# A fused attention and MLP kernel: one store of 128 rows a block, groups gated on the DMA turn, later squares, later casts of v, two more units of filler

## The chip, the cores and the metric

The kernel runs on one core of one Trainium2 chip. The metric is the device time of one execution in microseconds (us); smaller is better. The core has a matmul engine (PE, its weight loads are shown as PEld), a vector engine (DVE), an activation engine (ACT), GpSimd (POOL) and a sync engine (SP). Here SP issues every DMA, in its own order. "Clock" is the PE clock that the chip granted, as a share of full speed.

Runs carry a state. A run more than 1.5% above the fastest run of the same kernel counts as slow; a single run on one core is "unknown". On the chip of the first experiments the kernel before had three slow runs of seven (333 to 336 us), so medians over all its runs mislead there.

## The reference, cut to what matters

```python
# q, k, v: (8 batches, 8 heads, 576 rows, 64)
A, Bm, C = sm(q, k_lm), sm(q_lm, k_lm), sm(q_lm, k)       # landmarks: means of 18 rows
Z = Bm.T / (norm1(Bm) * norm_inf(Bm) + 1e-6)
for _ in range(6): Z = 2 * Z - Z @ Bm @ Z
x = (A @ Z @ C @ v)                                       # heads side by side: (8, 576, 512)
xn = (x - mean(x)) / sqrt(var(x) + 1e-6) * g_ln
out = x + relu(xn @ w_ch1) @ w_ch2                        # 512 -> 2048 -> 512
```

## The kernel before

The 4608 rows are 36 blocks of 128 rows, and 4 blocks are a group. The MLP of a group is 64 matmuls of 128x512 into "psh" (first product) and 64 into "pso" (second product). It is written as a generator; `fill(n)` takes n of its matmuls as filler between the small matmuls of the attention of later batches. Batches 0 and 1 go alone; then come four sets: batch 2, batches 3 and 4, batches 5 and 6, batch 7.

A block's way: its rows are made on DVE (`xblk`, with their sum); POOL makes the negative mean (`negm`) and the centred rows (`xn`); SP turns these by a DMA transpose into `xnT`, the operand of the first product. ACT takes the squares (`junk`) for the deviation, which is only needed when the second product is evicted.

Other names in the views: `stg` is a piece of q, k or v as loaded, `nat` and `natv` its casts to 16 bits (`natv` of v); POOL sums `nat` into `asum` and `s`; from DVE's sums `part` PE makes the landmarks (`psl`), which ACT copies out (`lm`); `psec` and `pscv` are products of the attention with them, `psn` is a step of the iteration for Z, and `psy` (from `zcbd`) gives the rows.

```python
def block_done(j):                          # groups 2 and up
    later.append(lambda: mean_of(j, pool))
    later.append(lambda: center(j, pool) ...)      # ends in the DMA transpose
    squares.append(lambda: square(j))              # one is taken out per step
    if u == 3: squares.append(lambda: deviations(g))   # ends in ln_ready.add(g)

def store(j, ot, cols):                     # two stores of 64 rows a block
    for i in range(2):
        b, c = divmod(2 * j + i, NJ)
        half = ot[ds(64 * i, 64), cols]
        to = out[b].rearrange("(t j) f -> j t f", j=NJ)[c][:, cols]
        nc.sync.dma_start(out=to, in_=half)

def mlp():
    for g in range(NGRP):
        ...
        while g > 1 and g not in ln_ready: yield False    # no filler until then
        ... 64 matmuls into psh, Relu on ACT ...
        ... 64 matmuls into pso, eviction on DVE, store ...
```

(Cut and joined for reading; "..." marks the cuts.) The 64 rows of a half block lie 9 rows apart in the output, and the two halves start in different places, sometimes in different batches.

The softmax here doesn't subtract the row's maximum and nothing guards it: scores larger than these inputs give would overflow.

Of the kernel before, what the change touches and what calls it, by code (L numbers as in the profile page):

```python
# [20 lines left out]
def kernel(  # L21
# [10 lines left out]
    nc = tc.nc  # L32
# [11 lines left out]
    NJ = 9  # L44
# [685 lines left out]

        yield from rows_of(bs, ea, zcbd)

    ln_ready = {0}
    rowsum, variances, rstds, xn_of = {}, {}, {}, {}
    mlp_at, uncentered = [0], {}
    later, squares, negms = [], [], {}

    def settle():
        while later:
# [2 lines left out]
    def block_done(j):  # L742
        g, u = divmod(j, 4)
        if g == 0:
            mean_of(j, dve)
            center(j, scalar if u % 2 == 0 else dve)
        elif g == 1:
            mean_of(j, dve)
            later.append(lambda: center(j, scalar))
        else:  # L750
            later.append(lambda: mean_of(j, pool))
            later.append(lambda: center(j, pool) if g <= mlp_at[0] + 1
                         else uncentered.setdefault(g, []).append(j))
        squares.append(lambda: square(j))
        if u == 3:
            if g == 1:
                later.append(lambda: ln_ready.add(1))
            squares.append(lambda: deviations(g))

    def mean_of(j, engine):  # L760
        negms[j] = mstat.tile([P, 1], FP32, name="negm", tag="negm", bufs=16)
# [3 lines left out]
    def center(j, engine):  # L765
        g, u = divmod(j, 4)
        xn_of[j] = xn = mxn.tile([P, DM], FP16, name="xn", tag="xn")
        if engine is scalar:
            act(xn[:], x_blk[j][:], AF.Identity, bias=negms[j][:], scale=1.0)
        elif engine is dve:  # L770
            dve.tensor_scalar(out=xn[:], in0=x_blk[j][:], scalar1=negms[j][:],
                              scalar2=None, op0=ALU.add)
        else:
            pool.tensor_scalar(out=xn[:], in0=x_blk[j][:], scalar1=1.0, scalar2=negms[j][:],
                               op0=ALU.mult, op1=ALU.add)
        if g < 2:
            return
        if u == 0:
            xnTs[g] = mxnT.tile([P, KCH, 512], FP16, name="xnT", tag="xnT")
        keep(nc.sync.dma_start_transpose(out=xnTs[g][:, :, ts(u, P)], in_=xn_of.pop(j)[:]))  # L780

    def square(j):
        g, u = divmod(j, 4)
# [6 lines left out]
    def deviations(g):  # L790
        lnv = mstat.tile([P, 4], FP32, name="lnv", tag="lnv")
        act(lnv[:], variances.pop(g)[:], AF.Ln, bias=eps_ln[:], scale=1.0 / DM)
        rstds[g] = mstat.tile([P, 4], FP32, name="rstd", tag="rstd")
        act(rstds[g][:], lnv[:], AF.Exp, scale=-0.5)
        ln_ready.add(g)

    def store(j, ot, cols):
        for i in range(2):
            b, c = divmod(2 * j + i, NJ)
            half = ot[ds(64 * i, 64), cols]  # L800
            to = out[b].rearrange("(t j) f -> j t f", j=NJ)[c][:, cols]
            nc.sync.dma_start(out=to, in_=half)

    xnTs = {}

# [19 lines left out]
    def mlp():  # L825
        for g in range(NGRP):
            mlp_at[0] = g
            hT = mhT.tile([P, MCH, 512], FP16, name="hT", tag="hT")
            if g == 0:
                for m0, u in ([(m, 0) for m in range(0, 12, 2)] + [(m, 2) for m in range(0, 12, 2)]  # L830
                              + [(m, u) for u in (0, 2) for m in (12, 14)]):
                    for t in {(0, 0): (0, 1), (8, 0): (2,), (10, 0): (3,)}.get((m0, u), ()):
                        transpose_block(0, t)
                        yield True
                    psh = psM.tile([P, 2, 256], FP32, name="psh", tag="pm")
                    for m in range(2):
                        for c in range(KCH):
                            MM(psh[:, m, :], w1_16[:, c, ts(m0 + m, P)],
                               xnTs[0][:, c, ds(P * u, 256)],
                               start=(c == 0), stop=(c == KCH - 1), skip=True)  # L840
                            if c == 1 or (c == 3 and m == 0):
                                yield True
                    act(hT[:, m0:m0 + 2, ds(P * u, 256)], psh[:], AF.Relu)
                    yield True
            else:
                while g == 1 and g not in xnTs:
                    if g in ln_ready:
                        for _ in transposes(g):
                            yield True
                    else:  # L850
                        yield False
                while g > 1 and g not in ln_ready:
                    yield False
                xnT = xnTs.pop(g)
                for j in uncentered.pop(g + 1, ()):
                    center(j, pool)
                for m in range(MCH):
                    psh = psM.tile([P, 512], FP32, name="psh", tag="pm")
                    for c in range(KCH):
                        MM(psh[:], w1_16[:, c, ts(m, P)], xnT[:, c, :],  # L860
                           start=(c == 0), stop=(c == KCH - 1))
                        if c < KCH - 1:
                            yield True
                    act(hT[:, m, :], psh[:], AF.Relu)
                    yield True
            tr = None
            for u in range(4):
                j = 4 * g + u
                x = x_blk.pop(j)
                ot = mout.tile([P, DM], FP32, name="ot", tag="ot")  # L870
                parts = 2 if j == NBLK - 1 else 1
                n = DM // parts
                for part in range(parts):
                    pso = psM.tile([P, n], FP32, name="pso", tag="pm")
                    for m in range(MCH):
                        MM(pso[:], hT[:, m, ts(u, P)], w2_16[:, m, ts(part, n)],
                           start=(m == 0), stop=(m == MCH - 1))
                        if m < MCH - 1:
                            yield True
                        if g == 0 and u >= 2 and m % 8 == 3:  # L880
                            if 1 in ln_ready and 1 not in xnTs:
                                tr = transposes(1)
                            if tr is not None:
                                next(tr, None)
                                yield True
                    dve.scalar_tensor_tensor(out=ot[:, ts(part, n)], in0=pso[:],
                                             scalar=rstds[g][:, u:u + 1], in1=x[:, ts(part, n)],
                                             op0=ALU.mult, op1=ALU.add)
                    store(j, ot, ts(part, n))
                    yield True  # L890
            if tr is not None:
                for _ in tr:
                    yield True
# [68 lines left out]
    def prepare(c, casts, jobs):  # L962
        for _ in range(casts):
            if c.casts and (c.parts[c.casts[0]][0] == "v" or len(c.n16) < 8):
                c.next_cast()
                while sum(len(x.stg) for x in sets) < (3):
                    left = [x for x in sets if x.loads]
                    if not left:
                        break
                    left[0].next_load()  # L970
        for _ in range(jobs):
            c.next_job()

    for _ in range(6):
# [1 line left out]

    fills = {"scores of k": 4, "gram": 5, "iteration": 4,
             "product": 5, "zc": 4, "rows": 6}
    def a_square():
        if squares:  # L980
            squares.pop(0)()

    n = 0
    for what in a1:
        fill(fills[what])
        settle()
        if what in ("iteration", "product"):
            a_square()
        if what in ("product", "zc", "rows"):
            n += 1  # L990
            prepare(sets[0], 1, 1 if n > 3 else 0)
    while len(sets[0].jobs) > 1:
        prepare(sets[0], 1, 1)
        fill(6)
    fill(16)

    steps = [[(10, 0), (12, 1)] + 6 * [(6, 1)] + [(8, 1)] + 5 * [(6, 0)]]
    steps += [[(6, 0), (8, 0), (12, 0), (12, 0), (6, 0), (6, 0), (5, 0), (5, 0), (5, 0), (5, 0), (8, 0)] + 3 * [(6, 0)] + 7 * [(7, 1)]]
    steps += [[(12, 0), (14, 1), (16, 1), (16, 1)] + 6 * [(9, 1)] + [(10, 1)] + 10 * [(8, 1)]]
    steps += [[(15, 0), (18, 0)] + 6 * [(12, 0)] + [(12, 0)] + 5 * [(12, 0)]]  # L1000
    for c, after, plan in zip(sets, sets[1:] + [None], steps):
        while c.jobs:
            prepare(c, 1, 1)
            fill(5 if c is sets[1] else 8)
        for (count, jobs), _ in zip(plan, attention2(c.bs, c)):
            fill(count)
            settle()
            a_square()
            if after:
                prepare(after, 1, jobs)  # L1010
    settle()
    while squares:
        a_square()
    for _ in stream:
        pass

# [29 lines left out]
```

## Time and profile before

| | before |
|---|---|
| median of its first 3 runs | 329.57 us (328.91 to 330.02) |
| span of the profile | 327.9 us |
| PE busy | 312.7 us, 95% |
| mean PE clock | 0.989 |
| last eviction to the end | 324.29 to 327.9: 3.6 us |

### The profile page before, as it was taken

To read this page: it belongs to the slowest core of one execution; us is meant where nothing else is said; L and a number is where in the kernel's file an instruction comes from. 1 tells how busy PE (TensorE), PEld (TensorE's weight loads), DVE (VectorE), ACT (ScalarE), POOL (GpSimd) and SP (SyncE) were. 2 spreads that over 40 slices of the span, in tenths; PEclk is the share of its full clock that TensorE was granted. 3 is DMA by queue.
4 is the path that set the end of the run, shared out by engine and by line. 5 is a ranking of instruction groups with operands and counts; after the bars stand their busy time and mean duration, and the time that the engine had idled before them with its cause. 6 is when DMAs were issued, how large, how long until landed. Compare 5 with 4: busy or idle time off the path is not lost.

```text
span 327.9 us, 7900 instructions
## 1 busy us (share of the span) xinstructions
PE 312.7 (95%) x3248; PEld 157.5 (48%) x3248; DVE 147.7 (45%) x392; ACT 153.9 (47%) x301; POOL 126.6 (39%) x194
## 2 busy tenths in 40 slices
PE   8789999899977989999999999999999999999994
PEld 8568654444432534544454445444444444444443
DVE  2667249678782415799366346431232210010012
ACT  2466853587043671567505644583048316305600
POOL 4389879708994796448043011600010300000000
PEclk9999999999995999999999999999999999999999
DMA  7999999559959993933086003520341124032023
GB/s 265 395 386 385 386 389 281 161 109 388 200 133 292 381 246 88 209 113 65 10 213 162 0 18 80 98 35 2 71 98 25 33 67 93 2 79 50 2 56 72
DMA packets 38700, 50.32 MB, mean 153 GB/s; under 512 B 17540, under 2 KB 17800, under 8 KB 38664
## 3 DMA queue, kind: packets, MB, share of 16 engines
q1 hardware_dynamic: 38664, 49.82, 53.6%
q8 instruction: 25, 0.41, 0.6%
q14 instruction: 11, 0.09, 0.1%
HBM read 36.70 MB, written 9.44 MB: 141 GB/s over the span
## 4 chain that ended last, share of the span: by engine, by line
PE 77%; POOL 6%; DMA 5%; DVE 5%; issue 2%; ACT 2%; SPq 1%; POOLq 0%
PE psh L73 35%; PE pso L73 31%; DMA stg<-in_k_dram 2%; PE psy L73 2%; POOL asum L67 2%; PE psn L73 2%; PE pscv L73 2%; DMA xnT<-xn 2%; POOL nat L67 1%; POOL natv L67 1%; DMA stg<-in_q_dram 1%; DVE xblk L67 1%; PE psec L73 1%; DVE part L67 1%; SPq L780 1%
## 5 line engine op out<-in xcount | busy, mean ns | idle before, releaser
L73 PE MATMUL psh<-xnT,w 128*128 128x512 f16 (+1 forms) x640 | 136.3, 360 | 2.0 <-DMA xnT<-xn 2.0
L73 PE MATMUL pso<-w,hT 128*128 128x512 f16 (+1 forms) x592 | 134.5, 375 | 0.0
L67 ACT ACTIVATE hT<-psh 128x512 f16<-128x512 f32 x144 | 85.0, 598 | 89.4 <-PE psh L73 88.8
L73 PEld LDWEIGHTS <-w 128*128 128x128 f16 x640 | 59.2, 98 | 60.5 <-issue 7.3
L73 PEld LDWEIGHTS <-hT 128*128 128x128 f16 x592 | 56.5, 98 | 58.1 <-issue 1.8
L67 DVE SCALAR_TENSOR_TENSOR ot<-pso,rstd,xblk 128x512 f32<-128x512 f32 (+1 forms) x37 | 27.1, 732 | 71.7 <-PE pso L73 68.4
L67 POOL CAST nat<-stg 128x1152 f16<-128x1152 f32 x28 | 31.6, 1145 | 33.4 <-DMA stg<-in_q_dram 30.0
L67 ACT ACTIVATE junk<-xblk,negm 128x512 f16<-128x512 f32 x36 | 25.9, 721 | 30.1 <-POOL negm L67 29.9
L67 POOL TENSOR_SCALAR negm<-rowsum 128x1 f32<-128x1 f32 x28 | 5.3, 190 | 76.8 <-DVE xblk L67 67.6
L67 DVE SCALAR_TENSOR_TENSOR xblk<-psy,rcpd 128x512 f32<-128x512 f32 (+1 forms) x40 | 27.6, 691 | 2.7 <-DVE rcpd L67 0.5
L67 DVE SCALAR_TENSOR_TENSOR st<-st,psn 128x128 f16<-128x128 f16 (+2 forms) x36 | 11.4, 316 | 38.3 <-PE psn L73 38.3
L67 POOL CAST natv<-stg 128x1152 f16<-128x1152 f32 x16 | 18.4, 1161 | 12.1 <-DMA stg<-in_v_dram 12.0
L67 POOL TENSOR_SCALAR xn<-xblk,negm 128x512 f16<-128x512 f32 x28 | 19.2, 692 | 2.0 <-DMA xnT<-xn 0.9
L67 DVE STREAM_TRANSPOSE xT<-nat 128x576 uint32<-128x576 uint32 x24 | 18.4, 768 | 0.0
L67 DVE TENSOR_REDUCE part<-xT 128x32 f16<-128x576 f16 x26 | 18.3, 745 | 0.1
L67 DVE RECIPROCAL rcpd<-psy 128x8 f32<-128x8 f32 (+1 forms) x40 | 8.1, 202 | 20.9 <-PE psy L73 20.8
L73 PE MATMUL psy<-zcbd,ea 128*128 128x260 f16 (+1 forms) x80 | 15.6, 276 | 0.6 <-DVE zcbd L67 0.5
L73 PEld LDWEIGHTS <-st 32*32 32x32 f16 x448 | 5.7, 89 | 16.7 <-issue 11.8
L67 POOL TENSOR_TENSOR asum<-asum 128x256 f32<-128x256 f32 (+1 forms) x22 | 13.0, 591 | 1.7
L67 POOL TENSOR_TENSOR asum<-nat 128x512 f32<-128x512 f16 x11 | 12.7, 1154 | 0.9
L73 PEld LDWEIGHTS <-ea 128*128 128x128 f16 (+1 forms) x80 | 7.2, 100 | 10.9 <-issue 2.6
L67 ACT ACTIVATE ec<-psec 128x576 f16<-128x576 f32 x12 | 8.9, 808 | 7.3 <-PE psec L73 7.3
(101 smaller groups left out, 210.3 us busy)
## 6 DMA issues: line engine op xcount, KB each, us to landing
stg<-in_q_dram SPq DMA_DIRECT2D x16, 576.0 KB, 7.4
stg<-in_k_dram SPq DMA_DIRECT2D x16, 576.0 KB, 7.5
out_dram<-ot SPq DMA_DIRECT2D x70, 128.0 KB, 2.3
wstg<-in_moe_w_ch_dram SPq DMA_DIRECT2D x16, 512.0 KB, 6.9
stg<-in_v_dram SPq DMA_DIRECT2D x10, 576.0 KB, 9.0
stg<-in_v_dram SPq DMA_DIRECT2D x12, 288.0 KB, 9.5
xnT<-xn SPq DMA_TRANSPOSE x28, 2.5
out_dram<-ot SPq DMA_DIRECT2D x4, 64.0 KB, 2.0
```

Source lines behind the costliest of these rows:

```text
L67: return lambda *args, **kw: keep(getattr(self.engine, op)(*args, **kw))
L73: keep(nc.tensor.matmul(o, l, r, start=start, stop=stop, tile_position=(rb, cb), skip_group_check=(skip or cb != 0)))
L780: keep(nc.sync.dma_start_transpose(out=xnTs[g][:, :, ts(u, P)], in_=xn_of.pop(j)[:]))
```

## The change

Its intent: fewer issues on SP (one store a block), a group's first product as soon as its rows are turned, squares out of the way of ACT's other work, and POOL free for the centring of batch 2.

```diff
-        squares.append(lambda: square(j))
+        squares.append((at[0], lambda: square(j)))
...
+        if u == 3:
+            turned.add(g)                    # after the fourth DMA transpose
...
     def store(j, ot, cols):
+        rows = []
         for i in range(2):
             b, c = divmod(2 * j + i, NJ)
-            half = ot[ds(64 * i, 64), cols]
-            to = out[b].rearrange("(t j) f -> j t f", j=NJ)[c][:, cols]
-            nc.sync.dma_start(out=to, in_=half)
+            rows.append(out[b].rearrange("(t j) f -> j t f", j=NJ)[c][:, cols])
+        both = bass.AP(rows[0].tensor, rows[0].offset,
+                       [[rows[1].offset - rows[0].offset, 2]] + [list(x) for x in rows[0].ap])
+        nc.sync.dma_start(out=both, in_=ot[:, cols])
...
-                while g > 1 and g not in ln_ready:
+                while g > 1 and g not in turned:
                     yield False
...                                           # before the second product:
+            while g not in rstds:
+                yield False
...
-    def a_square():
-        if squares:
-            squares.pop(0)()
+    def a_square(least=4):
+        at[0] += 1
+        if squares and at[0] - squares[0][0] >= least:
+            squares.pop(0)[1]()
...
-    fill(16)
+    fill(18)
...                                           # steps: (filler, casts, jobs); casts was always 1
+    steps = [[(10, 1, 0), (12, 1, 1)] + 6 * [(6, 1, 1)] + [(8, 1, 1)] + 5 * [(6, 0, 0)]]
+    steps += [[...] + 4 * [(5, 1, 0)] + [(8, 0, 0)] + 3 * [(6, 0, 0)] + 7 * [(7, 1, 1)]]
```

The output pattern of the new store is 2 places x 64 rows x 512 columns; on the chip's side it is 128 partitions x 512 columns.

More of the change, by code (lines that the diff above doesn't have):

```diff
@@ L731, in attention2 @@
         yield from rows_of(bs, ea, zcbd)
-    ln_ready = {0}
+    ln_ready, turned = {0}, set()
     rowsum, variances, rstds, xn_of = {}, {}, {}, {}
     mlp_at, uncentered = [0], {}
-    later, squares, negms = [], [], {}
+    later, squares, negms, at = [], [], {}, [0]
     def settle():
@@ L757, in block_done @@
                 later.append(lambda: ln_ready.add(1))
-            squares.append(lambda: deviations(g))
+            squares.append((at[0], lambda: deviations(g)))
     def mean_of(j, engine):
@@ L794, in deviations @@
         act(rstds[g][:], lnv[:], AF.Exp, scale=-0.5)
-        ln_ready.add(g)
     def store(j, ot, cols):
+        rows = []
         for i in range(2):
             b, c = divmod(2 * j + i, NJ)
-            half = ot[ds(64 * i, 64), cols]
-            to = out[b].rearrange("(t j) f -> j t f", j=NJ)[c][:, cols]
-            nc.sync.dma_start(out=to, in_=half)
+            rows.append(out[b].rearrange("(t j) f -> j t f", j=NJ)[c][:, cols])
+        both = bass.AP(rows[0].tensor, rows[0].offset,
+                       [[rows[1].offset - rows[0].offset, 2]] + [list(x) for x in rows[0].ap])
+        nc.sync.dma_start(out=both, in_=ot[:, cols])
     xnTs = {}
@@ L965, in prepare @@
                 c.next_cast()
-                while sum(len(x.stg) for x in sets) < (3):
+                while sum(len(x.stg) for x in sets) < 3:
                     left = [x for x in sets if x.loads]
@@ L987 @@
         if what in ("iteration", "product"):
-            a_square()
+            a_square(0)
         if what in ("product", "zc", "rows"):
@@ L994 @@
         fill(6)
-    fill(16)
-    steps = [[(10, 0), (12, 1)] + 6 * [(6, 1)] + [(8, 1)] + 5 * [(6, 0)]]
-    steps += [[(6, 0), (8, 0), (12, 0), (12, 0), (6, 0), (6, 0), (5, 0), (5, 0), (5, 0), (5, 0), (8, 0)] + 3 * [(6, 0)] + 7 * [(7, 1)]]
-    steps += [[(12, 0), (14, 1), (16, 1), (16, 1)] + 6 * [(9, 1)] + [(10, 1)] + 10 * [(8, 1)]]
-    steps += [[(15, 0), (18, 0)] + 6 * [(12, 0)] + [(12, 0)] + 5 * [(12, 0)]]
+    fill(18)
+    steps = [[(10, 1, 0), (12, 1, 1)] + 6 * [(6, 1, 1)] + [(8, 1, 1)] + 5 * [(6, 0, 0)]]
+    steps += [[(6, 1, 0), (8, 1, 0), (12, 1, 0), (12, 1, 0), (6, 1, 0), (6, 1, 0)] + 4 * [(5, 1, 0)] + [(8, 0, 0)] + 3 * [(6, 0, 0)] + 7 * [(7, 1, 1)]]
+    steps += [[(12, 1, 0), (14, 1, 1), (16, 1, 1), (16, 1, 1)] + 6 * [(9, 1, 1)] + [(10, 1, 1)] + 10 * [(8, 1, 1)]]
+    steps += [[(15, 0, 0), (18, 0, 0)] + 6 * [(12, 0, 0)] + [(12, 0, 0)] + 5 * [(12, 0, 0)]]
     for c, after, plan in zip(sets, sets[1:] + [None], steps):
@@ L1004 @@
             fill(5 if c is sets[1] else 8)
-        for (count, jobs), _ in zip(plan, attention2(c.bs, c)):
+        for (count, casts, jobs), _ in zip(plan, attention2(c.bs, c)):
             fill(count)
@@ L1009 @@
             if after:
-                prepare(after, 1, jobs)
+                prepare(after, casts, jobs)
     settle()
     while squares:
-        a_square()
+        a_square(0)
     for _ in stream:
```

## The prediction

> **What bounds the kernel now.** I read the page first, then the chain of waits in order of time, then what each engine waited for, then the timelines of PE, POOL, ACT and SP between 56 and 126 us.
>
> ```profile
> PE 312.7 (95%) x3248; PEld 157.5 (48%) x3248; DVE 147.7 (45%) x392; ACT 153.9 (47%) x301; POOL 126.6 (39%) x194
> ...
> PE   8789999899977989999999999999999999999994
> ```
>
> PE is the bound: 312.7 of 327.9 us. Only the missing 15.2 us, and time in which PE runs slowly, can be won. The windows put about 4.1 us of the 15.2 in the first 30 us (loads and warm-up, which the change leaves alone) and 4.1 at the very end. From 126.0 to 323.8 us PE is busy 197.77 of 197.80 us at clock 1.00. So there the change can lose, and not win. What is left lies between 56 and 126 us. All waits of PE there:
>
> ```profile
> PE psl L73 <- ACT lm L67: 2.7, 1, 2.7
> PE psh L73 <- DMA xnT<-xn: 2.0, 1, 2.0
> PE psn L73 <- issue: 1.4, 2, 1.1
> PE psl L73 <- DVE part L67: 0.9, 1, 0.9
> ```
>
> Columns: total us, times, longest. The first two fall at 95.9 to 98.6 and 100.3 to 102.3 us. They cost more than 4.66 us, as the windows show (PE busy, PEld, DVE, ACT, POOL, then PE clock):
>
> ```profile
> 96.00:98.50 2.50, 0.00 (x0) 0.10 (x1) 1.10 (x1) 1.77 (x6) 2.40 (x4) 1.00 1.09 262
> 98.50:100.30 1.80, 1.69 (x5) 0.63 (x5) 0.00 (x0) 0.62 (x2) 0.59 (x1) 0.58 1.05 335
> 100.30:102.25 1.95, 0.00 (x0) 0.00 (x0) 0.75 (x1) 0.00 (x0) 1.15 (x1) 0.50 1.05 171
> 102.25:105.60 3.35, 3.33 (x53) 1.14 (x53) 0.24 (x1) 1.09 (x2) 1.11 (x1) 0.50 1.07 382
> ```
>
> After the first gap the clock is halved. Work of 1.69 us at 0.58 and 3.33 us at 0.50 lost 0.7 + 1.7 = 2.4 us. By groups: psh x6 took 2.00 us instead of the 1.40 of its later twin, psec 0.96 instead of 0.52, psh x2 1.01 instead of 0.60, pso x3 1.47 instead of 0.65; together 2.3. I use 2.3.
>
> Why the two gaps: the chain of waits runs through SP and POOL.
>
> ```profile
> 65.77 0.63 DVE ot L67
> 66.95 0.59 SPq L802
> 67.65 2.72 SPq L780
> 70.43 4.57 DMA stg<-in_q_dram
> 75.05 1.16 POOL nat L67
> ...
> 89.79 1.10 POOL natv L67
> ...
> 91.80 1.16 POOL natv L67
> ...
> 93.85 1.16 POOL natv L67
> ...
> 95.90 1.16 POOL natv L67
> 97.12 5.11 DMA xnT<-xn
> 102.27 1.01 PE psh L73 x2
> ```
>
> SP held the load of q behind the stores of group 0's last block and one DMA transpose, so POOL had nothing to cast from 64.0 to 75.05. Late by that, it casts v between the centred rows of batch 2, which group 2's transposes need. ACT meanwhile stands in line: its squares ("junk") waited 12.4 us for POOL's negm in 80 to 100 us, and the copy of the landmarks (lm), done at 98.53, stood behind the last of them. That copy is what psl waited for.
>
> [...] The isolated gaps of 0.95 and 1.13 us cost no clock. [...] The add "part" took 1.21 us at 95.89, just beside the v cast at 95.90 to 97.06, and 0.19 at best.
>
> **The change part by part.**
>
> Two more units of filler before set 0's last landmark product (16 to 18). A unit is one 128x512 matmul, 13.81/64 = 0.216 us. PE waits 0.95 us there for DVE; 0.43 of it is filled: gain 0.43. More important, block 3's last matmul, now one unit after the scores of set 0, comes before them. Its eviction moves from 65.69 us to about 63.0, ahead of the softmax on DVE.
>
> One store a block. A store of 64 rows occupies SP 0.47 to 0.59 us; one of 128 rows needs one such issue, since loads onto 128 partitions take 0.37 to 0.57. That is 37 issues fewer, nearly all off the path. On it: one at 66.95, and one after the last eviction. With both parts SP sends the store at 63.8, the transpose (2.72) at 64.4, and the load of q at about 67.1 instead of 70.43: 3.3 us earlier. POOL is unbroken from there to 98 us, so its first v cast ends at 87.6 instead of 90.9.
>
> No v casts beside the rows of batch 2. Between the first centred block and the third (the last that group 2 needs) lie two casts, 2 x 1.16 = 2.3 us. Now the three blocks follow each other at 0.95 us (0.19 + 0.69 + gaps) and end at about 90.4 instead of 96.0. The loads that went with the casts also leave SP. The last transpose of group 2, issued at 97.12 and landed at 102.2 before, is issued at about 91 and lands by 95 with the 4 us that it takes here. PE wants it at about 96.5. Gain: 2.00. The casts come back in the next stretch, where POOL has nothing else to do until loads arrive, and before v is used.
>
> Squares four steps later. The first square of batch 2 then stands behind three more steps, with its negm long there; the lm copy is free to run after its matmul. The psl at 98.58 then waits only for DVE's "part". That ended at 97.10; without the v cast beside it the add takes about 0.3 instead of 1.21, and everything is 0.43 earlier: about 95.8, where PE arrives at 95.5. Gain 2.66 - 0.3 = 2.36.
>
> The gate on the turn. Group 2's and 3's first products may start before their deviations, and the second product waits for the deviations (emitted two to six steps later, against 64 units of first product). It makes room for the later squares; by itself it gains nothing.
>
> The clock: with at most 0.3 us of idleness there, none of the 2.3 us is lost: gain 2.3. The tail: the eviction ends at 324.29, two issues take 1.10, landing 2.0: one issue less gains 0.5.
>
> Sum: 0.43 + 2.00 + 2.36 + 2.3 + 0.5 = 7.6 us, so 322.0. The two "issue" gaps (1.4 us) I leave. Since two of these terms depend on times that I moved by hand, I take 322.2.
>
> **Rivals.**
>
> First, another wait takes the place of psl's. DVE is nearly unbroken from 88.7 to 97.1. If "part" is no quicker (1.21 again, another POOL cast beside it), psl still waits about 1.2 us: 323. If the stores are still placed before the last transpose of group 2, that waits for an eviction at about 96.5 and lands near 100: 3 us of waiting and half the clock loss stay, 326. For it: before, one transpose (103.10) did stand behind stores that waited for DVE. Against: that was the first of group 3, after a late POOL.
>
> Second, the gain is given back later. PE has no idle time after 126, but little room: before set 2's second psl at 156.99 DVE's "part" was ready at 156.23, and group 3's last transpose (issued at 136.92, 1.70 long, then 2.5 to land) met a PE that wanted it at 141.64. The change takes v casts from the rows before that transpose, but puts two beside busy DVE rows afterwards. If DVE loses 1 us there, PE waits a few tenths: 322.5 to 323.5.
>
> Third, store traffic or SP were never on the path, so that the 3.3 us don't come. Then POOL still wins 2.3 us, xnT lands near 98.5, PE waits about 1.5 us and perhaps keeps some clock loss: 325.
>
> A gain above mine: the "issue" gaps close too, 320.5.
>
> **Range and chances.** The recoverable idle time and clock loss are 7.0 + 2.3 + 0.5 = 9.8 us, a floor of about 319.8. The rivals reach 326. I take 320.0 to 325.0. Two per cent faster is about 323.0, 0.8 us above my number; rivals one and two end beside that line, three above it: 0.63 faster, 0.36 within, 0.01 slower (no part adds work to PE).
>
> **What would show it.** Right: no PE wait over 1 us between 60 and 120 us, PE clock 1.00 in all slices, the load of q issued near 67, group 2's last transpose landed before 96, lm copies right after their psl, PE unbroken from some 120 us to the end, 37 stores. Wrong: a wait of psh for xnT that remains, a clock digit below 9 near 100 us, new PE waits at the landmarks of sets 2 and 3, or SP holding loads behind an eviction as long as before.

## More of the kernel before

The page gives PE's busy share in 40 slices of 8.2 us. The prediction reads the rest: PE is the bound, and nearly all its idle time that the change can reach lies between 56 and 126 us. Two lines that the prediction did not show turned out to matter, the DMA lines of that picture, share of 16 engines and GB/s:

```profile
DMA  7999999559959993933086003520341124032023
GB/s 265 395 386 385 386 389 281 161 109 388 200 133 292 381 246 88 209 113 65 10 213 162 0 18 80 98 35 2 71 98 25 33 67 93 2 79 50 2 56 72
```

From about 180 us on, where little but stores and transposes moves, the engines are at most half busy, and there are slices in which next to nothing moves: the stores are soon done.

## The result, and the profile after

| | before | after |
|---|---|---|
| median of 4 runs | 329.79 us (328.91 to 333.28) | 367.81 us (366.02 to 368.56) |
| span of the profile | 327.9 us | 366.8 us |
| PE busy | 312.7 us | 318.8 us |
| mean PE clock | 0.989 | 0.942 |
| last eviction to the end | 3.6 us | 14.2 us |

The ratio is 1.112 (95% interval 1.103 to 1.122): 11% slower, where 2.2% faster was predicted. Ratios here are the mean time of one kernel's fast runs over that of the other's of the same rounds, so they are not quite the ratio of the medians quoted.

The page after, PE, its clock and the DMA lines:

```profile
PE   8989999983949989429999999969999999999930
...
PEclk9999999996996999858999999989999999999985
DMA  7999995499565899999325915470186019111011
GB/s 278 396 384 387 386 292 189 66 131 350 142 80 207 68 329 231 142 168 76 51 83 151 74 47 56 65 75 0 40 64 73 21 51 86 36 51 45 21 51 42
```

A slice is 9.2 us here. PE now has holes near 85, 105, 155 and 243 us, and the last two slices hold little. The DMA share over the whole span rose although the bytes are the same:

```profile
q1 hardware_dynamic: 37554, 49.82, 61.9%
```

(packets, MB, share of 16 engines' span; before, the page has 53.6% of a shorter span). The waits of PE (total us, times, longest), which answer those of the prediction:

```profile
PE psh L73 <- DMA xnT<-xn: 16.7, 2, 12.6
PE psy L73 <- DVE zcbd L67: 7.8, 2, 7.3
PE pscv L73 <- issue: 3.0, 1, 3.0
PE psl L73 <- DVE part L67: 1.5, 2, 1.0
```

psl no longer waits for ACT's lm, as predicted. But psh waits for transposes more than before, 4.1 us near 108 and 12.6 us near 157. The window of the tail, with nothing but stores left (PE, PEld, DVE, ACT, POOL, clock, DMA share, GB/s), says how the stores move:

```profile
352.70:365.00 12.30, 0.00 (x0) 0.00 (x0) 0.00 (x0) 0.00 (x0) 0.00 (x0) 0.58 0.13 50
```

A share of 0.13 is 2 of 16 engines (0.125), and 50 GB/s is 25 GB/s for each. The packets in the trace agree: in this window two are under way for 10.7 of the 12.3 us, and never fewer. One store of 256 KB (262,144 bytes) then takes 5.2 us. In a second product PE makes a block every 16 x 0.216 = 3.5 us. So the stores fall behind: the last group's first block is evicted near 342.5 us, its four blocks need 4 x 5.2 = 21 us, and the end cannot come before 363.5.

Upstream, the slow stores stand in front of everything that SP sends. The chain of waits at the place where the prediction had the load of q go out at 67.1 us:

```profile
67.34 6.98 SPq L780
74.37 8.06 DMA stg<-in_q_dram
82.48 1.16 POOL nat L67
```

The eviction that releases SP did start early, at 62.5 us. But the third store was then in issue for 3.55 us (63.25 to 66.80) and the first transpose for 6.98, instead of 0.5 and 1.3 to 2.7. (The two stores just before it took 0.54 and 0.55 us, so the issue itself cost what was predicted.) SP's timeline has the third store:

```profile
63.25 3.55 SPq L805 DMA_DIRECT2D out_dram<-ot  x1
```

The load of q goes out at 74.4 and takes 8.1 us. From there the lateness passes through POOL to DVE and to PE, which waits 7.29 us for zcbd, since DVE stands at a transpose of rows that POOL has not cast.

### The profile page after: what moved, and what is told of

It reads as the page before. It is cut to its first block, busy times and chain, and to the rows that moved or that the text cites. A ratio compares the mean times of both kernels' runs of the same rounds, so it can differ in the third digit from the quotient of the medians.

```text
span 366.8 us, 7853 instructions
## 1 busy us (share of the span) xinstructions
PE 318.8 (87%) x3248; PEld 158.9 (43%) x3248; DVE 148.6 (41%) x392; ACT 153.6 (42%) x301; POOL 126.5 (34%) x194
## 4 chain that ended last, share of the span: by engine, by line
PE 70%; DMA 9%; POOL 7%; DVE 5%; issue 3%; SPq 2%; ACT 1%; POOLq 0%
PE psh L73 33%; PE pso L73 26%; DMA xnT<-xn 4%; DMA stg<-in_q_dram 2%; POOL asum L67 2%; DMA stg<-in_k_dram 2%; PE psy L73 2%; SPq L780 2%; POOL natv L67 2%; PE psn L73 1%; PE pscv L73 1%; POOL nat L67 1%; DVE xblk L67 1%; PE psec L73 1%; DVE part L67 1%
## 5 line engine op out<-in xcount | busy, mean ns | idle before, releaser
L73 PE MATMUL psh<-xnT,w 128*128 128x512 f16 (+1 forms) x640 | 140.6, 368 | 16.7 <-DMA xnT<-xn 16.7
L73 PEld LDWEIGHTS <-w 128*128 128x128 f16 x640 | 60.0, 100 | 77.8 <-DMA out_dram<-ot 12.8
L67 POOL CAST natv<-stg 128x1152 f16<-128x1152 f32 x16 | 18.3, 1162 | 16.6 <-DMA stg<-in_v_dram 10.6
L73 PE MATMUL psy<-zcbd,ea 128*128 128x260 f16 (+1 forms) x80 | 16.4, 286 | 7.9 <-DVE zcbd L67 7.8
L67 DVE STREAM_TRANSPOSE ecT<-ec 128x288 uint32<-128x288 uint32 x12 | 5.5, 466 | 16.0 <-ACT ec L67 15.7
```

The costliest lines, as they stand in the source:

```text
L67: return lambda *args, **kw: keep(getattr(self.engine, op)(*args, **kw))
L73: keep(nc.tensor.matmul(o, l, r, start=start, stop=stop, tile_position=(rb, cb), skip_group_check=(skip or cb != 0)))
```

## The experiments

Theory A after the result: the whole loss is the new store. It runs on 2 engines (a DMA share of 0.13 in the tail), and the transposes and loads that stand behind it are held up (a transpose 6.98 us in issue, a load of q 8.06 us under way, 4.57 before). That the outermost count of 2 in its output pattern makes it so was not shown yet. Rival B: the new order (gate, late squares, late casts) costs too.

**Two stores a block again, the rest of the change kept.**

```diff
 (changed kernel)
-        nc.sync.dma_start(out=both, in_=ot[:, cols])
+        the store of the kernel before, two of 64 rows
```

> The changed kernel with the two stores of 64 rows a block of the kernel before; the rest of the change stays. Theory A (the loss is all in the store of 128 rows, which moves its 256 KB at some 50 GB/s on about 2 of 16 engines, and holds up the transposes and loads that stand behind it there): the rest of the change works as predicted, 321.5 to 324 us, no psh wait for xnT, PE clock 1.00 from 60 to 300 us, the end after the last eviction back to 3.6 us from 14. Theory B (the new order, gate on the turn, late squares, late casts, also costs): above 333 us with PE waiting for xnT or zcbd still.

Measured: 324.52 us median (323.03 to 325.36, 4 runs); the fast runs of before 328.26 to 332.95; ratio 0.982 (0.969 to 0.996). No psl or psh wait between 61 and 102 us, 3.6 us from the last eviction to the end. PE's only wait of note is another one (start, length, engine, operation, idle time before it):

```profile
105.69 0.30 PE L73 MATMUL pscv<-natv,ecT 64*32 64x65 f16 x26 [2.91 <-issue]
```

Theory A holds for the time, and B falls. The loss against this run splits into three parts: the waits of PE add up to 32.8 us after and 8.0 here (24.8 more), PE is busy 318.8 against 310.8 us (8.0 more, at a mean clock of 0.942 against 0.993), and the tail is 14.2 against 3.6 us (10.6). Together that is 43.4 us, the difference of the spans, 366.8 - 323.4. Waits, busy time and tail make up nearly all of any span, so that the sum closes proves nothing; the sizes of the parts are what it shows.

**The kernel before with nothing but the new store.**

```diff
 (kernel before)
-    two stores of 64 rows
+    the store of the changed kernel
```

> The kernel before with nothing changed but the store, one of 128 rows a block. Theory A: 355 to 372 us, a DMA share near 0.13 while only stores are under way, about 14 us from the last eviction to the end. Theory B: most of the loss comes from the new order, so within 8 us of the kernel before plus the slow end (330 to 348).

Measured: 371.14 us (369.88 and 372.41); ratio 1.125. In a window of its tail the DMA share is 0.13 and the rate 50 GB/s; 14.3 us from the last eviction to the end. The store alone costs all of it. The changed kernel's median is 3.3 us lower, so the rest of the change seems to win a little even under the slow store, but the two were run in different rounds.

**62 and 2 rows, and 48 and 16 rows.** These runs ask what about the store is slow. Theory A in its sharp form takes the number of engines to go with what divides the row count of a store; nothing measured so far had shown that. Both cut each half block into two plain stores, so that no pattern has a third dimension with a count of 2 and none crosses into another place.

```diff
 (changed kernel)
+            for r0, n in ((0, 62), (62, 2)):     # control: ((0, 48), (48, 16))
+                nc.sync.dma_start(out=to[r0:r0 + n, cols], in_=ot[ds(64 * i + r0, n), cols])
```

> The changed kernel, each half block stored in two transfers of 62 and 2 rows, both plain patterns without the outer dimension of 2. Theory A in its sharp form [...]: as slow as the changed kernel, 355 to 375, DMA share near 0.13 beside stores, slow end. Rival C (the outer dimension of 2, or 256 KB in one transfer, or rows of two places in one transfer, is slow by itself): as fast as the run with 48 and 16 rows, under 335.

> The control of the run with 62 and 2 rows: the same four transfers a block, but 48 and 16 rows, both divisible by 16. Theory A: [...] 321 to 331 us, slower than two stores a block only by the SP time of two more issues a block (0.5 us each). Rival D (four issues a block are what makes the 62 and 2 run slow): as slow as that run.

Measured: 361.83 us (361.64 and 362.02) with 62 and 2 rows, 327.27 (325.65 and 328.89) with 48 and 16. The window of the 62 and 2 run's tail:

```profile
345.70:356.00 10.30, 0.00 (x0) 0.00 (x0) 0.00 (x0) 0.00 (x0) 0.00 (x0) 0.66 0.13 50
```

Again 2 engines and 50 GB/s, with transfers of 124 KB that have no third dimension. Rivals C and D fall: neither the third dimension, nor the 256 KB, nor four issues a block make it slow. 62 is 2 x 31 and 48 is 3 x 16.

**61 and 3 rows, and 63 and 1.** The sharp form makes an odd forecast: 61 is a prime and 63 is 7 x 9, so one row fewer should be much worse, one row more should be harmless.

```diff
 (the 62 and 2 run)
-            for r0, n in ((0, 62), (62, 2)):
+            for r0, n in ((0, 61), (61, 3)):     # other run: ((0, 63), (63, 1))
```

> As the run with 62 and 2 rows, with 61 and 3: one row fewer in the long transfer. [...] Estimate from the changed kernel: 2 engines moved some 50 GB/s, so one moves 25, and 36 blocks x 2 x 61 rows x 2 KB = 9.0 MB take 360 us on it from 51 us on, with its share of the loads: above 420 us. Rival C (62 rows are slow for a reason that has nothing to do with divisors, such as a short second transfer): 355 to 370 like 62 and 2.

> As the runs with 62+2 and 61+3 rows, with 63+1. [...] this run, whose long transfer is longer than both, is as fast as 48+16: 324 to 331 us. Rival C (uneven cuts are slow, the more so the shorter the rest): as slow as 62+2 or slower, above 355.

Measured, one run each (state unknown): 489.70 us with 61 and 3 rows, 323.66 with 63 and 1. The tail of the first:

```profile
450.00:480.00 30.00, 0.00 (x0) 0.00 (x0) 0.00 (x0) 0.00 (x0) 0.00 (x0) 0.50 0.07 26
```

A share of 0.07 is one engine (0.0625), at 26 GB/s. 63 rows in one transfer are as good as 64 in the run with two stores (323.66 and 324.52 us). So in these runs the number of engines went with what divides the row count, not with the size: 61, 62, 63 and 64 rows, on 1, 2, 9 and 16 engines, gave 490, 362, 324 and 325 us. A rule for other counts is not shown. The packets of the kept traces give these counts. In the tails of the 61 and 3 run and of the 62 and 2 run at least 1 and 2 packets are under way at any time and seldom more. From 250 to 320 us, of the times with more than one packet under way, the longest has 9 of them with 63 and 1 rows (6.4 us) and 16 in the two-store run (5.4 us).

**Which part of the rest carries the gain?** Five runs take the other parts apart. The prediction gave each part its own term of a sum.

```diff
 (two stores a block)                                     run
-    def a_square(least=4):      +    def a_square(least=0):      squares at once
-    5 * [(6, 0, 0)]             +    5 * [(6, 1, 0)]             casts back
-    [(8, 0, 0)] + 3 * [(6, 0, 0)]  +  [(8, 1, 0)] + 3 * [(6, 1, 0)]  (casts back, second place)
-    fill(18)                    +    fill(16)                    16 units
 (both of the first two)                                  both back
 (kernel before)  -    fill(16)  +    fill(18)            before with 18 units
```

> The run with two stores a block, but the squares again as soon as they are queued (age 0 instead of 4). Prediction's step: the late squares free the copy of the landmarks, and with them psl, worth up to 2.36 us and part of the clock loss. Theory E (each part carries its own gain): psl waits 1.5 us or more for ACT's lm near 96 us, 326 to 329 us. Rival F (with v's casts out of the way POOL gives negm in time, so the squares no longer block ACT): no psl wait above 0.7 us, 322 to 325.5, the same as with late squares.

> The run with two stores a block, but v is cast beside the rows of batch 2 and of the first rows of batch 3 as before. Prediction's step: the two casts between the centred blocks delay group 2's last transpose by 2.3 us. The load of q is some 3.6 us earlier than in the kernel before, so the transpose should land near 98 with PE there at 96.4. Theory E: psh waits 1 to 2 us for xnT near 97 us, 324.5 to 327. Rival F: the earlier load alone has made room, no wait of psh above 0.3 us, 322 to 325.5.

> Squares at once and v's casts back: of the change only the gate, and 18 instead of 16 units of filler, are left. Theory E: psl waits for ACT's lm again (squares behind negm behind casts), 1 to 2.5 us, and psh for xnT about 1 us: 326 to 330. Rival F (the two units of filler, which bring the last store of group 0 and so the load of q forward, are most of it): 322.5 to 326.

> The run with two stores a block, with 16 units of filler before set 0's last landmark product instead of 18; gate, late squares and late casts stay. If the two units of filler are what frees the load of q (theory F from the last runs), block 3's store is sent near 66.4 us again, the load of q after 69 instead of 66.8, and xnT is late or only just in time at 96 us: 325 to 328. If the other parts suffice (theory E): no wait of psl or xnT above 0.5 us, 323 to 325.5.

> The kernel before with 18 instead of 16 units of filler and nothing else. Theory F: the load of q near 67 us instead of 70.4, psl without the wait for ACT's lm, at most 2 us of waiting for xnT near 97 us, clock not halved between 98 and 106 us: 323.5 to 326.5, as the run with squares and casts back. Theory E: the squares still block lm, 327 to 329.5.

| run | median (range), us | ratio (95%) | psl wait | psh wait, group 2 |
|---|---|---|---|---|
| two stores a block | 324.52 (323.03 to 325.36) | 0.982 (0.969 to 0.996) | none | none |
| squares at once | 324.23 (323.91 to 325.62) | 0.985 (0.979 to 0.992) | none | none |
| casts back | 326.39 (326.17 to 330.36) | 0.994 (0.982 to 1.007) | 0.93 | 2.12 |
| both back | 324.66 (324.48 to 327.05) | 0.988 (0.979 to 0.996) | 0.25 | 1.98 |
| 16 units | 323.65 (322.38 to 324.50) | 0.986 (0.981 to 0.991) | 0.68 | none |
| before with 18 units | 325.91 (325.24 to 326.48) | 0.993 (0.989 to 0.998) | 0.20 | 2.87 |

The waits (us, near 96 to 99) are of one profile each (that of "casts back" is of its slowest run, 330.36), and the psl waits are all for DVE's part. For instance, before with 18 units:

```profile
95.77 0.39 PE L73 MATMUL psl<-part,spread 128*128 128x256 f16 x2 [0.20 <-DVE part L67]
99.25 1.87 PE L73 MATMUL psh<-xnT,w 128*128 128x512 f16 x4 [2.87 <-DMA xnT<-xn]
```

Theory E falls for the squares and for the filler. With 18 units alone the last store of group 0 leaves before the scores, the load of q goes out at 66.76 us, POOL is early, and the squares find their negm in time: ACT's lm is not blocked although the squares come at once. With 16 units and the rest of the change lm is not blocked either, although the load of q goes out at 69.45 us instead of 66.82. So the terms for the filler and for the squares are not two gains that add up. Which of the late squares, the late casts and the gate stands in for the filler there, no run separates. E holds for the casts as a wait: wherever v is cast beside the rows, psh waits 2.0 to 2.9 us for group 2's transpose, and in the three runs without those casts it doesn't. As time it is not shown: "both back" has the wait, and is no slower than the rest. The other runs with two stores differ too little (323.65 to 324.66, their ranges overlap) to rank; by their ratios "casts back" and "before with 18 units" lie higher, with 0.993 to 0.994 against 0.982 to 0.988, but the intervals overlap. The prediction's second rival, a gain given back later at group 3's transposes, shows in part: near 136 us psh waits 1.25 us for one with 16 units, and 1.19 and 1.82 us in the runs of 48 and 16 and of 63 and 1 rows, but not in the run with two stores.

**Fewer loads in flight.** The profile of each of these six runs has 0.6 to 3.0 us left in which PE waits for nothing that it shows ("issue"), between 102 and 122 us.

```diff
 (two stores a block)
-                while sum(len(x.stg) for x in sets) < 3:
+                while sum(len(x.stg) for x in sets) < 2:
```

> The run with two stores a block, with 2 instead of 3 staged loads kept under way. Every fast run so far has 1.4 to 3 us in which PE waits for nothing that the profile shows ('issue'), between 102 and 123 us, where the DMA share is 1.0 and PE runs its many small matmuls. Theory G (PE's instructions come late because loads fill the DMA engines): with fewer loads in flight the gap shrinks below 0.7 us, 321 to 323 us, if no new wait for casts comes. Rival H (the gap has nothing to do with the loads): it stays at 1.4 to 3 us, 323 to 326.

Measured: 328.78 us (326.70 to 330.00, 6 runs); ratio 1.002 (0.998 to 1.006). The "issue" wait is gone in its profile, as G says, but a new wait takes its place:

```profile
139.05 3.17 PE L73 MATMUL psh<-xnT,w 128*128 128x512 f16 x7 [6.51 <-DMA xnT<-xn]
```

POOL gets its rows of batches 5 and 6 later: it sums and casts them until 131.6 us and only then centres the blocks of group 3, the last at 134.5, where the two-store run had done so at 130.9. G is supported by one profile, not settled: with the loads the whole order of the next 20 us moved. As a change it loses: 1.002 against 0.982 to 0.988 for most of the runs with three loads. One more thing in the kept traces speaks for G. The page's "instruction" queue q8 moves packets of 16 KB. In before and in every run with fast stores, all eleven "issue" waits between 102 and 124 us end 1.2 to 1.7 us after such a packet has landed. That PE stood waiting for its next instructions is not shown by this: it is a coincidence in time, and no experiment; four of the five such waits under slow stores have no such packet within 6 us before their end.

## Why the prediction was wrong

**The step that failed** is "One store a block": "one of 128 rows needs one such issue", "37 issues fewer, nearly all off the path". I counted what the store costs its issuer, took the transfer itself as unchanged, and never worked out how it would be spread. The runs put this in its place: about 5.2 us a store on 2 engines (worked out from 50 GB/s), 3.55 us and 6.98 us of SP at the place where 0.5 was to be saved, 14.2 us after the last eviction instead of 3.1. My tail term of +0.5 us measured -10.6. The profile of before held a warning: a store of 128 KB landed in 2.3 us (part 6 of the page, below), which is 57 GB/s from issue to landing, while loads moved close to 390 GB/s in slices with a DMA digit of 9, some 24 for each of 16 engines: by this estimate a store on 2 engines, at 48, would have had to be slower than that. On how many engines the new store would run, the profile of before does not show.

```profile
out_dram<-ot SPq DMA_DIRECT2D x70, 128.0 KB, 2.3
```

**How the runs had the stores spread**: 2 x 64 rows at a DMA share of 0.13, 62 rows at 0.13, 61 rows at 0.07; 64, 48 + 16 and 63 + 1 rows without such a loss (324.52, 327.27 and 323.66 us).

**The third rival** asked whether stores and SP were on the path at all, and answered "then 325". It looked only for a smaller gain. None of my rivals let a part of the change be worse than what it replaced, hence the 0.01 for slower: "no part adds work to PE" was true, and beside the point, for PE waits for what DMA brings.

**The clock** fell after the first gap alone. The prediction counts its loss with both gaps ("They cost more than 4.66 us"), but its own windows have the clock at 0.58 between 98.50 and 100.30 us, so it had fallen after the first gap (2.66 us) and before the second began. In before with 18 units a single gap of 2.87 us did the same (0.50 from 99 to 102 us), and so did 2.91 us with two stores (0.50 from 107 to 110 us). With casts back it was 0.50 from 101 to 103 us after a gap of 2.12 us (and one of 0.93 shortly before it), and after one of 2.15 us five psh matmuls took 2.31 us instead of 1.25. With 48 and 16 rows twelve psh matmuls took 4.45 us instead of 2.76 after a gap of 1.56 us. Gaps of 1.66 us (63 and 1 rows), 1.98 (both back) and 2.11 (squares at once) left the clock at 1.00 from 94 to 112 us, so the length of the gap alone does not decide.

**What was right**, seen without the new store (the two-store run):

- Block 3's eviction "to about 63.0": 62.66 us. The load of q "at about 67.1": 66.82, although one more store stood before it, because the first transpose took 1.33 us instead of 2.72.
- No psh wait for group 2's transpose; psl at 95.77 us without a wait, predicted 95.8. The add "part" took 0.20 us, where 1.21 beside a cast was feared to remain.
- PE clock 1.00 from 56 to 104 us.
- The sum: without its store terms (0.5) it was 7.1 us. The spans differ by 4.5 (327.9 and 323.4). The "issue" time, which I left as it was, took 2.91 us instead of 1.40 (1.5 more), and after it PE ran at 0.50 from 107 to 110 us (1.5 more). 7.1 - 3.0 = 4.1; the other 0.4 I assign to nothing.

**What was right only in the sum**: the 2.36 us for the late squares is no term of its own, for 18 units alone also free psl, and so does the rest of the change with 16 units. The 2.00 for the casts is one, as a wait: 2.0 to 2.9 us wherever the casts stand beside the rows.

The faster version is therefore the change with its old store: 324.5 us, against 328.3 to 333.0 for the fast runs of before beside it. Whether it is over 2% stays open (interval 0.969 to 0.996).

## What to carry to other kernels

When two DMAs are joined into one, find out on how many engines the joined one runs before counting the issues saved: a window of the profile in which nothing else moves shows it. Here 2 x 64 and 62 rows had a DMA share of 0.13 and 61 rows 0.07, while stores of 64, of 48 and 16 and of 63 and 1 rows cost no such time. A store is not free because nobody waits for it: here the transpose behind it was 6.98 us in issue instead of 1.3 to 2.7, and the load of q behind that left at 74.4 us instead of 66.8. And when several parts of a change feed one wait, ask of each whether it still gains with the others in place, before adding the terms up.
